# Expert stage of a fused attention and mixture kernel: first-layer sums on three rotating PSUM banks, the second layer's chain a with one alternating bank

## The chip, the cores and the metric

The kernel runs on one core of a Trainium2 chip. The metric is the device time of one execution in microseconds (us). Each time is the median of several executions; one further execution is profiled, and everything that is said of single instructions comes from that one.

## What is computed

Three stages follow one another: an attention in which a query sees only keys of its own cluster, a dense two-layer block with softplus, and a mixture of eight experts whose weights come from a Sinkhorn normalisation. All is float32. The change is in the last stage, cut here to what matters:

```python
def _moe2_ref(x, w_gate, w1, w2):            # x: 1536 x 512, 8 experts, w1[e]: 512 x 1024
    logits = x @ w_gate
    P = np.exp(logits - logits.max())
    for _ in range(8):
        P /= P.sum(1, keepdims=True) + 1e-09
        P /= P.sum(0, keepdims=True) + 1e-09
        P *= N / E
    for e in range(E):
        h = np.maximum(x @ w1[e], 0.0)
        out += P[:, e:e + 1] * (h @ w2[e])
```

## The kernel before

Each float32 operand is split into a high and a low part, and each product is made of three matmuls (high x high, high x low, low x high). On top of that both layers of an expert use a 2 x 2 block scheme with seven products in place of eight (the table `PROD`), so that sums of blocks are formed before and after.

**Stages.** Up to about 600 us the attention and the dense block run, after that the expert stage. In it the 1536 tokens are two halves of 768; the eight experts run over the first half and then over the second, so there are 16 passes, called experts 0 to 15 here (`k` in the code).

**First layer** (`l1_group`). An expert has four quarters `u`, and a quarter has seven groups, i = 0 to 6, in the order of `PROD`. A group is 6 matmuls of 128 x 128 weights with 384 columns. The groups add into two PSUM chains: chain a takes i = 0, 2, 4, 6, chain b takes i = 1, 3, 5, and i = 3 starts chain b afresh. Between the groups the sums are read: ScalarE copies after i = 0, 2, 3 (line 919, the tiles c0 and c2), VectorE adds after i = 1, 4, 5 (line 929), and a ScalarE Relu after i = 6 (line 927). In the profile chain a is called `l0m`, chain b `l1m` while it holds i = 1 and `l3m` from i = 3 on. A group that adds into a chain has to wait until the reader of the group before is done, and a group that starts a chain has to wait until the last reader of its bank is done.

**Second layer** (`l2_piece`). An expert has 14 steps (seven products, each in two halves p), a step has three pieces t = 0, 1, 2 of 128 tokens, a piece has 6 matmuls with 256 columns. The pieces add into chains a and b again (`Ya0m`, `Ya1m`, `Yb0m`, `Yb1m` in the profile; the digit 0 is the bank of t = 0 and 1, the digit 1 that of t = 2, the tail block). After the second half of a product VectorE scales the sums and adds them to the output (lines 961 and 963); for chain a this is after i = 0, 2, 4, 6, for chain b after i = 1, 3, 5.

**Banks.** PSUM has eight banks. `ps_l` holds `la` and `lb`, one for each chain of the first layer; `ps_y` holds `y0` to `y5`. The second layer's chain a uses y0 and y1 in even experts, y2 and y3 in odd ones; chain b uses y4 and y5. In expert 0, whose second layer has not begun, the first layer's odd quarters use y4 and y5. The gate (`gate`, `gate_max`, `sinkhorn`), which runs during expert 0, uses y2 and y3 for its small results.

**Order.** A list `ev2` of steps with due times is sorted and executed in that order when the kernel is built. The second layer of expert k runs beside the first layer of expert k + 1: one and a half pieces follow each group. Between groups i and i + 2 there are three pieces and one group. The framework then lays out each engine's queue from these steps, by priority and by when a step can run in its own reckoning, and sets the semaphores; copies and adds out of PSUM have a raised priority. Each engine works its own queue in order. VectorE has further work there: sums of blocks (`g_sum`, line 72 and 74), low parts of the hidden values (`g_split`, line 889) and of the weights (`w1_split`, line 840). ScalarE casts the high parts (lines 888, 867, 839). POOL forms the low parts of the second layer's weights (`w2_split`, line 868) and issues some DMAs (line 210).

The part that the change touches most, before it:

```python
if i in (0, 1, 3):
    if k == 0 and v:
        LB[bank] = ps_y.tile([P, FH], F32, tag={"a": "y4", "b": "y5"}[bank], name="l" + nm)
    else:
        LB[bank] = ps_l.tile([P, FH], F32, tag="l" + bank, name="l" + nm)
```

Of the kernel before, what the change touches and what calls it, by code (L numbers as in the profile page):

```python
# [7 lines left out]
F32 = mybir.dt.float32  # L8
# [12 lines left out]
def attention_moe_moe2(ctx, tc, v, qt, kt, centroids, w_in, w_out, w_gate, w1, w2, eye, out, dbg=None):  # L21
# [5 lines left out]
    E = w_gate.shape[1]  # L27
    FE = w1.shape[2]
    P = 128
    NT = S // P  # L30
    HT = NT // 2
    CB = HT * P
# [550 lines left out]
    for i in range(NHALF):  # L583
        g = i // 4
        for t in range(HT):
            n = 6 * i + 2 * t - LEAD
# [6 lines left out]
        for s in range(NT):  # L593
            n = 6 * i + s
# [36 lines left out]
    ps_l = ctx.enter_context(tc.tile_pool(name="ps_l", bufs=1, space=PSUM))  # L631
    ps_y = ctx.enter_context(tc.tile_pool(name="ps_y", bufs=1, space=PSUM))
    FH = S // 2
# [39 lines left out]
    Y = {}  # L673
# [39 lines left out]
    def gtile(shape, tag, b, nm):  # L713
        return ps_y.tile(shape, F32, tag=tag, name=nm) if b else ps_l.tile(shape, F32, tag="lb", name=nm)

    def gate(b, hf):
        lg = gtile([E, CB], f"y{2 + hf}", b, f"lg{b}{hf}")
        for c in range(KC):
            nc.tensor.matmul(
                lg, wg[:, c, :], xt[b][:, c, hf * CB : (hf + 1) * CB], start=c == 0, stop=c == KC - 1  # L720
            )
        if b:
            ls = slot_pool["gp"].tile([E, CB], F32, tag="gl", name=f"ls{b}{hf}", bufs=4)
        else:
            ls = slot_pool["fp"].tile([E, CB], F32, tag="u", name=f"ls{b}{hf}", bufs=2)
        nc.scalar.copy(ls, lg)
        tp = gtile([P, HT, E], f"y{2 + hf}", b, f"lgT{b}{hf}")
        for t in range(HT):
            nc.tensor.transpose(tp[:, t, :], ls[:, t * P : (t + 1) * P], idf[:E, :E])
        nc.vector.tensor_copy(lt[:, b * NT + hf * HT : b * NT + (hf + 1) * HT, :], tp)  # L730
# [3 lines left out]
    def gate_max(ph):  # L734
        if ph == 0:
            nc.vector.tensor_reduce(sm[:, 0:1], lt.rearrange("p t e -> p (t e)"), AX.X, ALU.max, negate=True)
            tp = ps_y.tile([1, P], F32, tag="y2", name="gmT")
            nc.tensor.transpose(tp, sm[:, 0:1], idf)
            g1 = mp.tile([1, 1], F32, tag="g1", name="g1", bufs=1)
            nc.vector.tensor_reduce(g1, tp, AX.X, ALU.min)  # L740
            G["g1"] = g1
            return
        bp = ps_y.tile([P, 1], F32, tag="y3", name="gmB")
        nc.tensor.matmul(bp, ones_f[0:1, :], G["g1"], start=True, stop=True)
        nc.vector.tensor_copy(sm[:, 1:2], bp)
        nc.scalar.activation(Pt, lt, AF.Exp, bias=sm[:, 1:2], scale=1.0)

    def sinkhorn(it, ph):
        n = B * NT
        if ph == 0:  # L750
            rs = mp.tile([P, n], F32, tag="rs", name=f"rs{it}", bufs=1)
            nc.vector.tensor_reduce(rs, Pt, AX.X, ALU.add)
            nc.vector.tensor_scalar(rs, rs, 1e-9, None, ALU.add)
            nc.vector.reciprocal(rs, rs)
            nc.vector.tensor_tensor(Pt, Pt, rs.unsqueeze(2).to_broadcast([P, n, E]), ALU.mult)
            cs = G["cs"] = mp.tile([P, E], F32, tag="cs2", name=f"cs{it}", bufs=1)
            nc.vector.tensor_reduce(cs, Pt.rearrange("p t e -> p e t"), AX.X, ALU.add)
            return
        cs = G["cs"]
        cp = ps_y.tile([P, E], F32, tag=f"y{2 + it % 2}", name=f"cp{it}")  # L760
        nc.tensor.matmul(cp, ones_f, cs, start=True, stop=True)
        nc.vector.tensor_scalar(cs, cp, 1e-9, float(E) / N, ALU.add, ALU.mult)
        nc.vector.reciprocal(cs, cs)
        nc.vector.tensor_tensor(Pt, Pt, cs.unsqueeze(1).to_broadcast([P, n, E]), ALU.mult)
        if it == 7:
            nc.vector.tensor_scalar(Nt, Pt, -1.0, None, ALU.mult)
# [34 lines left out]
    W1U, XG, GH, WH, YA = {}, {}, {}, {}, {}  # L801
# [90 lines left out]
    LB = {}  # L892

    def l1_group(k, u, i):
        xn, wn, bank = PROD[i]
        p, v = divmod(u, 2)
        nm = f"{i}m{k}_{u}"
        if i in (0, 1, 3):
            if k == 0 and v:
                LB[bank] = ps_y.tile([P, FH], F32, tag={"a": "y4", "b": "y5"}[bank], name="l" + nm)  # L900
            else:
                LB[bank] = ps_l.tile([P, FH], F32, tag="l" + bank, name="l" + nm)
        ps = LB[bank]
        hi, lo = XC[f"2_{k // E}", xn]
        wh, wl, s_ = W1U[k, u][wn]
        n, nk = 0, KC // 2
# [8 lines left out]
        if i in (0, 2, 3):  # L915
            tag = "c2" if i == 2 else "c0"
# [4 lines left out]
        name = {1: "A11", 4: "A22", 5: "A12", 6: "A21"}[i]  # L921
# [11 lines left out]
    def l2_piece(k, i, p, t):  # L933
        sb, e = divmod(k, E)
        ch = PROD[i][2]
        if p == 0 and t == 0 and i in (0, 1, 3):
            o = 4 if ch == "b" else 2 * (k % 2)
            YA[ch] = [ps_y.tile([P, 512], F32, tag=f"y{o + n}", name=f"Y{ch}{n}m{k}_{i}") for n in range(2)]
        y = YA[ch]
        ps = y[t // 2][:, t % 2 * 256 : t % 2 * 256 + 256]  # L940
        (gh, gl), (wh, wl) = GH[k, i, p], WH[k, i, p]
# [12 lines left out]
        for t_ in ((0, 1) if t == 1 else (2,)):  # L954
            m = r * HT + t_
# [51 lines left out]
    for k in range(NB):  # L1007
# [26 lines left out]
        for i in range(7):  # L1034
            b, i_ = divmod(7 * k + i - 3, 7)
            do(split_at[b][2 * i_ + 1] + 0.15 if b >= 0 else -1, w2_load, k, i)
        for j in range(14):
            i, p = divmod(j, 2)
# [21 lines left out]
    for n, u in enumerate(m1):  # L1060
# [22 lines left out]
        if final:  # L1083
            for hf in range(2):
                gate(0, hf)
# [51 lines left out]
```

## Time and profile before

| | before |
|---|---|
| median of three runs | 1608.32 us (1608.15 to 1611.47) |
| the profiled execution | 1613.91 us |
| its span, first to last instruction | 1612.1 us |
| TensorE matmuls: busy, count | 1518.6 us (94%), 9873 |
| VectorE busy | 1244.7 us (77%) |
| ScalarE busy | 1006.5 us (62%) |
| POOL busy | 725.5 us (45%) |
| mean granted TensorE clock | 0.979 |

How to read it: PE is TensorE's matmuls and PEld its weight loads, DVE is VectorE, ACT is ScalarE. Matmuls are pipelined and their ends are modelled, so the busy time of PE says little; the distance between the starts of two matmuls says when TensorE stood. A wait is given as "engine line waited for: us in total, times, longest". L910 is line 910 of the kernel: the first layer's matmuls; L945 are the second layer's.

### The profile page before, as it was taken

How to read it: one execution, taken by the hardware profiler on the slowest of the kernel's cores; microseconds unless marked ns; L12 is line 12 of the kernel's file. 1: busy time of each engine (PE TensorE's matmuls, PEld its weight loads, DVE VectorE, ACT ScalarE, POOL GpSimd, SP SyncE). 2: the span in 40 equal slices, each digit the busy share in tenths (PEclk: the TensorE clock that was granted, in tenths of full speed). 3: DMA queues.
4: the chain of work that ended last, by engine and by line, in shares of the span. 5: the costliest groups of instructions: out<-in, count | busy, mean ns of one | idle time of the engine just before them, and what ended most of it. 6: DMA issues, size and time to landing. Idle time of an engine off the chain costs nothing. (4 is left out here: it accounts for less than half of the span.)

```text
span 1612.1 us, 26967 instructions
## 1 busy us (share of the span) xinstructions
PE 1518.6 (94%) x9873; PEld 1442.9 (90%) x9873; DVE 1244.7 (77%) x1826; ACT 1006.5 (62%) x1854; POOL 725.5 (45%) x546
## 2 busy tenths in 40 slices
PE   5889999898998999999999999999999999999998
PEld 4778888797988967899999999998999999999998
DVE  4899999865655356977887887898878878878877
ACT  3788888665555535556655665665566666666663
POOL 2322323433323125555665565565445445545544
PEclk7999999899999999999999999999999999999999
DMA  8555520499998406888988887533544443443422
GB/s 220 143 148 140 135 65 6 128 242 248 249 253 227 112 16 173 213 208 223 244 219 218 214 235 209 154 105 112 160 121 123 125 125 118 125 132 110 128 72 79
DMA packets 268532, 253.01 MB, mean 157 GB/s; under 512 B 12272, under 2 KB 235632, under 8 KB 268400
## 3 DMA queue, kind: packets, MB, share of 16 engines
q1 hardware_dynamic: 242656, 217.67, 44.5%
q0 software_dynamic: 25600, 33.56, 12.9%
q8 instruction: 77, 1.26, 0.3%
q14 instruction: 55, 0.45, 0.1%
q10 hardware_dynamic: 144, 0.07, 0.0%
HBM read 194.10 MB, written 36.70 MB: 143 GB/s over the span
## 5 line engine op out<-in xcount | busy, mean ns | idle before, releaser
L868 POOL TENSOR_TENSOR vl<-w2r,vh 128x512 fp32r<-128x512 f32 x224 | 362.3, 1620 | 410.7 <-ACT vh L867 406.3
L889 DVE TENSOR_TENSOR gl<-XA,gh 128x768 fp32r<-128x768 f32 x160 | 175.4, 1096 | 81.9 <-ACT gh L888 81.8
L888 ACT CAST gh<-XA 128x768 fp32r<-128x768 f32 x160 | 134.1, 838 | 108.9 <-PE Ya1m L945 94.5
L945 PE MATMUL Ya0m<-vh,gl 128*128 128x256 f32 x512 | 144.2, 282 | 0.7 <-DVE gl L889 0.7
L867 ACT CAST vh<-w2r 128x512 fp32r<-128x512 f32 x224 | 137.7, 615 | 10.3 <-PE y L688 6.7
L945 PE MATMUL Ya0m<-vh,gh 128*128 128x256 f32 x512 | 144.0, 281 | 0.0
L945 PE MATMUL Ya0m<-vl,gh 128*128 128x256 f32 x512 | 143.9, 281 | 0.0
L210 POOL DMA_DIRECT2D ts<-in_moe_w_dram x48 | 61.9, 1330 | 108.6 <-DMA ts<-in_moe_w_dram 33.9
L945 PE MATMUL Yb0m<-vh,gh 128*128 128x256 f32 x384 | 108.5, 283 | 2.4 <-DVE x L963 2.4
L945 PE MATMUL Yb0m<-vl,gh 128*128 128x256 f32 x384 | 108.6, 283 | 2.0 <-POOL vl L868 2.0
L548 DVE TENSOR_TENSOR el<-t,eh 128x384 fp32r<-128x384 f32 x192 | 102.6, 550 | 10.0 <-ACT eh L544 8.8
L509 DVE TENSOR_REDUCE sc<-s 128x1 f32<-128x768 f32 x96 | 91.2, 951 | 23.4 <-PE s L501 23.2
L945 PE MATMUL Yb0m<-vh,gl 128*128 128x256 f32 x384 | 108.8, 283 | 0.4 <-DVE gl L889 0.4
L931 ACT ACTIVATE XA<-XA 128x768 f32<-128x768 f32 x96 | 81.3, 847 | 38.9 <-DVE XA L929 38.9
L544 ACT CAST eh<-t 128x384 fp32r<-128x384 f32 x192 | 91.6, 481 | 21.4 <-PE t L541 12.3
L541 PE MATMUL t<-idf,E 128*128 128x128 f32 x576 | 97.6, 276 | 4.7 <-ACT OHT L449 2.8
L945 PEld LDWEIGHTS Ya0m<-vh,gl 128*128 128x128 f32 x512 | 97.0, 189 | 1.1 <-DVE gl L889 1.1
L945 PEld LDWEIGHTS Ya0m<-vh,gh 128*128 128x128 f32 x512 | 96.8, 189 | 0.0
L945 PEld LDWEIGHTS Ya0m<-vl,gh 128*128 128x128 f32 x512 | 96.8, 189 | 0.0
L514 ACT ACTIVATE E<-s,sc 128x768 f32<-128x768 f32 x96 | 87.2, 909 | 14.7 <-DVE sc L509 13.6
L72 DVE TENSOR_TENSOR XS<-XA,XA 128x768 f32<-128x768 f32 x32 | 63.9, 1998 | 32.3 <-ACT XA L927 32.3
L541 PEld LDWEIGHTS t<-idf,E 128*128 128x128 f32 x576 | 73.1, 142 | 14.5 <-ACT OHT L449 3.6
(252 smaller groups left out, 5311.8 us busy)
## 6 DMA issues: line engine op xcount, KB each, us to landing
w2r<-td SPq DMA_DIRECT2D x64, 512.0 KB, 4.0
w2r<-in_moe_w_dram SPq DMA_DIRECT2D x56, 512.0 KB, 4.2
ts<-in_moe_w_dram POOLq DMA_DIRECT2D x48, 512.0 KB, 7.7
td<-ts SPq DMA_DIRECT2D x48, 512.0 KB, 5.7
wf<-td SPq DMA_DIRECT2D x64, 256.0 KB, 3.9
w1r<-td SPq DMA_DIRECT2D x64, 256.0 KB, 3.4
AT<-HL SPq DMA_DIRECT2D x64, 192.0 KB, 4.0
ts<-in_moe_w_dram SPq DMA_DIRECT2D x24, 512.0 KB, 6.0
```

The costliest lines, as they stand in the source:

```text
L72: eng.tensor_tensor(out_, a, b, op)
L509: nc.vector.tensor_reduce(SC[i][:, 0, j, t : t + 1], Et[i, t][:, :, 0:CB], AX.XY, ALU.max, negate=True)
L514: nc.scalar.activation(e.rearrange("p (a c) -> p a c", a=2), Et[i, t][:, :, 0:CB], AF.Exp, bias=sc[:, 0, j, t : t + 1], scale=1.0, accum_o ...
L541: nc.tensor.transpose(pt[:, t * P : (t + 1) * P], Et[i, t][:, s * P : (s + 1) * P], idf)
L544: nc.scalar.copy(eh, TT[i, s])
L548: nc.vector.tensor_tensor(el, TT.pop((i, s)), EHL[i, s].bitcast(F32), ALU.subtract)
L867: nc.scalar.copy(h, src)
L868: nc.gpsimd.tensor_tensor(l, src, h.bitcast(F32), ALU.subtract)
L888: nc.scalar.copy(h, src)
L889: nc.vector.tensor_tensor(l, src, h.bitcast(F32), ALU.subtract)
L931: nc.scalar.activation(t, t, AF.Relu, scale=1.0 if name == "A11" else -1.0)
L945: nc.tensor.matmul(ps, g[:, v, ts], w[:, v, :], start=i in (0, 1, 3) and p == 0 and v == 0 and n == 0 and t != 1, stop=p == 1 and v == 1 a ...
```

## The change

Three edits in the expert stage:

- The first layer's sums take one of three banks, `la`, `lb` and `y1`, each time a chain is started. The place is counted on: within a quarter i = 0, 1 and 3 take three banks one after the other, and the next quarter begins one bank further. Expert 0 does the same.
- The second layer's chain a has y0 in even and y2 in odd experts for its first two blocks, and y3 for the tail block in every expert. Chain b stays on y4 and y5.
- The small results of the gate and the normalisation move from y2 and y3 to y4 and y5.

```diff
     def gate(b, hf):
-        lg = gtile([E, CB], f"y{2 + hf}", b, f"lg{b}{hf}")
+        lg = gtile([E, CB], f"y{4 + hf}", b, f"lg{b}{hf}")
...
-        tp = gtile([P, HT, E], f"y{2 + hf}", b, f"lgT{b}{hf}")
+        tp = gtile([P, HT, E], f"y{4 + hf}", b, f"lgT{b}{hf}")
...
-            tp = ps_y.tile([1, P], F32, tag="y2", name="gmT")
+            tp = ps_y.tile([1, P], F32, tag="y4", name="gmT")
...
-        bp = ps_y.tile([P, 1], F32, tag="y3", name="gmB")
+        bp = ps_y.tile([P, 1], F32, tag="y5", name="gmB")
...
-        cp = ps_y.tile([P, E], F32, tag=f"y{2 + it % 2}", name=f"cp{it}")
+        cp = ps_y.tile([P, E], F32, tag=f"y{4 + it % 2}", name=f"cp{it}")
...
         if i in (0, 1, 3):
-            if k == 0 and v:
-                LB[bank] = ps_y.tile([P, FH], F32, tag={"a": "y4", "b": "y5"}[bank], name="l" + nm)
-            else:
-                LB[bank] = ps_l.tile([P, FH], F32, tag="l" + bank, name="l" + nm)
+            tag = ("la", "lb", "y1")[(4 * k + u + (0, 1, 0, 2)[i]) % 3]
+            LB[bank] = (ps_y if tag == "y1" else ps_l).tile([P, FH], F32, tag=tag, name="l" + nm)
...
         if p == 0 and t == 0 and i in (0, 1, 3):
-            o = 4 if ch == "b" else 2 * (k % 2)
-            YA[ch] = [ps_y.tile([P, 512], F32, tag=f"y{o + n}", name=f"Y{ch}{n}m{k}_{i}") for n in range(2)]
+            tags = ("y4", "y5") if ch == "b" else (("y0", "y2")[k % 2], "y3")
+            YA[ch] = [ps_y.tile([P, 512], F32, tag=g, name=f"Y{ch}{n}m{k}_{i}") for n, g in enumerate(tags)]
```

## Rows read from the trace of the kernel before

**Rows 1.** The page: granted TensorE clock in 40 equal slices, tenths of full speed.

```profile
PEclk7999999899999999999999999999999999999999
```

**Rows 2.** Windows, one regular expert; columns: length, busy (x count) per engine, PEclk, DMA.

```profile
1212.73:1272.82 60.09, 60.02 (x421) 59.23 (x420) 48.67 (x64) 38.09 (x66) 30.04 (x21) 1.00 0.41 123
```

**Rows 3.** Waits of TensorE's weight loads, 600 us to the end.

```profile
PEld l3m L910 <- DVE XA L929: 19.4, 32, 3.1
PEld l0m L910 <- ACT XA L927: 7.8, 29, 1.5
```

**Rows 4.** Timeline of TensorE, expert 10, third quarter; columns: start, duration, engine, operation.

```profile
1242.59 0.28 PE L945 MATMUL Yb0m<-vh,gh 128*128 128x256 f32 x1
1242.87 0.45 PE L910 MATMUL l0m<-chA,whAm 128*128 128x384 f32 x1
1243.15 0.34 PE L910 MATMUL l0m<-clA,whAm 128*128 128x384 f32 x1
1243.33 0.34 PE L910 MATMUL l0m<-chA,wlAm 128*128 128x384 f32 x1
...
1248.94 0.28 PE L945 MATMUL Ya0m<-vl,gh 128*128 128x256 f32 x1
1249.06 0.28 PE L945 MATMUL Ya0m<-vh,gl 128*128 128x256 f32 x1
1249.31 0.44 PE L910 MATMUL l3m<-chS,whBm 128*128 128x384 f32 x1
```

**Rows 5.** Windows of 2 us behind the long stall in expert 4.

```profile
874.00:876.00 2.00, 2.00 (x9) 2.00 (x8) 2.00 (x3) 0.52 (x1) 0.00 (x0) 0.50 0.16 42
```

**Rows 6.** Timelines, expert 10: VectorE's add of i=4, TensorE's start of i=6.

```profile
1252.82 1.74 DVE L889 TENSOR_TENSOR gl<-XA,gh 128x768 fp32r<-128x768 f32 x1 [0.23 <-ACT gh L888]
1254.66 0.56 DVE L929 TENSOR_TENSOR XA<-l0m,c03m 128x384 f32<-128x384 f32 x1
1255.38 0.35 PE L910 MATMUL l0m<-chA,whCm 128*128 128x384 f32 x1
...
1224.28 0.54 DVE L929 TENSOR_TENSOR XA<-l0m,c03m 128x384 f32<-128x384 f32 x1
1225.38 0.34 PE L910 MATMUL l0m<-chA,whCm 128*128 128x384 f32 x1
```

**Rows 7.** Timelines of VectorE and TensorE around the stalls in experts 4 and 2.

```profile
864.06 5.13 DVE L72 TENSOR_TENSOR XS<-XA,XA 128x768 f32<-128x768 f32 x1 [2.45 <-ACT XA L927]
873.43 0.69 PE L910 MATMUL l3m<-chS,whBm 128*128 128x384 f32 x1 [2.88 <-DVE XA L929]
878.21 1.42 DVE L889 TENSOR_TENSOR gl<-XA,gh 128x768 fp32r<-128x768 f32 x1 [1.38 <-ACT gh L888]
879.73 0.56 DVE L929 TENSOR_TENSOR XA<-l0m,c03m 128x384 f32<-128x384 f32 x1
880.78 0.34 PE L910 MATMUL l0m<-chA,whCm 128*128 128x384 f32 x1
...
718.75 0.44 PE L910 MATMUL l3m<-chS,whBm 128*128 128x384 f32 x1 [1.90 <-DVE XA L929]
723.46 0.56 DVE L929 TENSOR_TENSOR XA<-l0m,c03m 128x384 f32<-128x384 f32 x1 [0.65 <-PE l0m L910]
```

**Rows 8.** Timelines: eviction of the tail block and next write to one.

```profile
1213.00 0.47 DVE L961 TENSOR_SCALAR x<-Ya1m,Pt 128x256 f32<-128x256 f32 x1
1215.93 0.28 PE L945 MATMUL Ya1m<-vh,gh 128*128 128x256 f32 x1
...
1085.62 0.28 PE L945 MATMUL Ya1m<-vh,gh 128*128 128x256 f32 x1
1086.65 0.47 DVE L963 SCALAR_TENSOR_TENSOR x<-Ya1m,Pt,x 128x256 f32<-128x256 f32 x1
1092.98 0.38 PE L945 MATMUL Yb0m<-vl,gh 128*128 128x256 f32 x1 [2.04 <-POOL vl L868]
```

**Rows 9.** The page's costliest groups: VectorE's sums of blocks.

```profile
L72 DVE TENSOR_TENSOR XS<-XA,XA 128x768 f32<-128x768 f32 x32 | 63.9, 1998 | 32.3 <-ACT XA L927 32.3
```

## Prediction, made before the changed kernel was run

> **What bounds the kernel now.** I read the page first: TensorE's granted clock is full almost everywhere from 600 us on [rows 1]; an engine kept at that clock hardly rests, so I take the time after 602 us (the expert stage, 1010 us of 1612) for TensorE's, and what can be won there for holes in its row. Next the table of windows, cut at the last Relu (L927) of each expert: one expert takes 60.1 us where nothing disturbs it [rows 2]. Next the timeline of TensorE: undisturbed, a 256-column matmul starts 0.12 us after its predecessor (0.118 over many of them) and a 384-column one 0.17 to 0.18 (0.174) [rows 4]. An expert has 42 x 6 = 252 of the first kind and 28 x 6 = 168 of the second: 252 x 0.118 + 168 x 0.174 = 59.0 us. So a regular expert loses 60.1 - 59.0 = 1.1 us; irregular ones lose up to 7. Last the view of waits, for TensorE's weight loads, which see every stall: the largest sum is i=3 waiting for the VectorE add (L929), 19.4 us in 32 places; next i=0 waiting for the ScalarE Relu (L927), 7.8 us in 29 [rows 3]. Both are waits for a bank, not for data: i=3 needs bank b, which the add of i=1 still reads, and i=0 of the next quarter needs bank a, which the Relu of i=6 still reads.
>
> That view gives the idle time; in starts a stall costs a little more, since the matmul behind it is late too. At 1242.87 the first matmul of i=0 comes 0.28 after its predecessor in place of 0.12, and the second 0.28 later in place of 0.17 [rows 4]: 0.16 + 0.11 = 0.27, where the weight load idled 0.21. Adding 0.07 for each of the 61 places: 19.4 + 7.8 + 4.2 = 31.4 us. The two stalls at 719 and 873 us are followed by some 3 us at half clock (0.50 in 874 to 876 us [rows 5]), where 384-column matmuls start 0.32 apart in place of 0.17: 1.6 and 1.3 us more. **All that the change could remove is so about 34 us.** TensorE's other waits (for data, for POOL, for the second layer's evictions) stay.
>
> **The change, part by part.** *First layer over three banks.* No instruction is added or removed, on any engine. The bank of i=0 is now the one that i=1 used a quarter before, free for most of that quarter; that of i=1 is the one of i=3 and i=5, the same distance as now; that of i=3 is the one of i=0 to i=6 of the quarter before, four groups ago. So the waits of i=0 for the Relu and of i=3 for the add go. Inside a quarter i=6 still waits for the add of i=4 (same chain), and i=2, i=4 and i=5 for ScalarE's copies. **What is late next** is VectorE, which works its queue in order: if it is behind, TensorE now runs on through i=3, i=4, i=5 and meets it at i=6. A removed stall counts only as far as i=6 can come earlier: by the distance from the end of i=4's add to the start of i=6, plus the time that VectorE idled before that add for something that TensorE itself sets free.
>
> Regular experts, third quarter: i=3 starts at 1249.31, 0.25 after its predecessor in place of 0.12 [rows 4], and with the matmul behind it loses 0.25; with i=0 that is 0.52. The add of i=4 ends at 1254.66 + 0.56 = 1255.22 and i=6 starts at 1255.38, so 0.16 is free, and VectorE idled 0.23 before, for a ScalarE cast whose buffer second-layer matmuls set free [rows 6]: 0.39 of 0.52 is kept. First quarter: its two stalls are the rest of the 1.1 us, 0.6; the add of i=4 ends at 1224.82, i=6 starts at 1225.38, VectorE is back to back [rows 6]: 0.56 is kept. The other quarters show no stall. The timeline has the first pattern in 10 experts and the second in 11: 10 x 0.56 + 11 x 0.39 = 9.9 us.
>
> Irregular stalls: the rest, 34.3 - (10 x 0.62 + 11 x 0.52) = 22.4 us, in thirteen places. They come where VectorE is late by itself: the subtraction at 864.06 takes 5.13 us, and i=3 then stands 2.88 us, until 873.43. There i=6 could come 880.78 - 880.29 = 0.49 earlier, plus VectorE's idle 1.38 at 878.21 [rows 7]: 1.9 of 4.2 us (with i=0 and the half clock). At 718.75 (1.90 us idle) VectorE afterwards waits for the matmuls of i=4, 0.65 [rows 7], and i=6 has 2.3 us to spare: nearly all, 3.0 us. At 630 and 906 us VectorE runs back to back up to the add of i=4: nothing, and 0.55. The bounds are 0 and 22.4; the same reading at all thirteen gives 13.1, and I take that.
>
> *Second layer's chain a with one alternating bank.* Its tail block (t=2) now sits in one bank for all experts, so its first matmul waits for VectorE's eviction of the expert before. Today that eviction ends at 1213.47 and the next tail matmul starts at 1215.93 [rows 8]: 2.46 us of cover, 2.2 when TensorE no longer stops at i=0. Eleven of the 15 boundaries have 2.4 or more, one 1.7, one 11. Two have none: at 1085.62 the matmul starts 1.5 us before the eviction ends (1086.65 + 0.47), and at the last expert 0.8. Behind the first comes a wait of 2.04 us for POOL at 1092.98 [rows 8], whose end POOL's own queue sets, so that the delay is hidden; without that cover it costs 1.5. Bounds 0 to 2.3; I take 0.8, the second alone. Queued behind that wait on TensorE is its own stream alone.
>
> *Expert 0 and the gate.* Its odd quarters had two banks of their own and now share the three; there the add of i=5 ends 1.0 us or more ahead of the i=1 that will need its bank, so nothing is added. The small tiles of gate and normalisation move to the banks of chain b, which starts after the last of them: 0, and at most one small VectorE step, under 1 us, were it not so.
>
> **Sum.** 9.9 + 13.1 - 0.8 = 22.2 us. The profiled execution took 1613.9 us (span 1612.1, 1.8 around it): 1591.7 for such a one. The median of the runs is 1608.3, 5.6 lower. What can differ between executions are irregular stalls, 38 us of the 56 that all starts after 602 us lose against 0.118 and 0.174; so I scale their term by 33/38 to 11.3: 20.4 us off the median, **1588 us**.
>
> **The rivals.** (B) VectorE takes back all that is irregular: where it is late, it is late until i=6. For it: 630 and 906 us. Against it: VectorE idles before the add of i=4 in most other places. Then 9.9 - 0.8 = 9: 1599 us. (C) All bank waits vanish, since an earlier TensorE also sets VectorE's inputs free earlier: 34 less, 1574 us. (D) The stalls only move to i=6, regular quarters too, or the build holds the banks as long as before: 1607 us. Against it: the free 0.16 to 2.3 us there. (E) The shared tail bank decides. The order of each queue is laid out anew at build time (today four second-layer matmuls stand ahead of i=0 that the program has behind it). If at an expert's end the eviction came behind two of the subtractions that now follow it, 2.0 us each by the page's mean [rows 9], TensorE would stand 4.0 - 2.2 = 1.8 us at 15 boundaries: 27 us against the 21 that the first layer gives, 1615 us. It decides from an eviction 3.6 us later than now. Against it: today's stands right behind its matmuls' other evictions. (F) More switching between banks makes TensorE's clock swing. In the trace TensorE changes banks at each group, and the granted clock is 1.00 through a whole regular expert [rows 2]; it fell behind the stalls of about 2 us or more alone [rows 5]. If each of the 64 quarters had one stretch like that, 1.3 us, it would cost 83: 1671 us. The Trainium skill has such a rule (TensorE: Matmul & The Clock Gate, section "A second HAM failure mode: psum-queue depth-cycling"): a kernel that cycles through PSUM banks each iteration idles briefly between groups of matmuls, often enough that the clock goes back and forth. The trace does not bear that out for the idles of 0.2 us here.
>
> **Chances.** Forecast 0.52, B 0.20, C 0.10, D 0.08, E 0.07, F 0.03. The range runs from C to a little past B, 1574 to 1603, and leaves out D, E and F: 0.18. A measurement of this kernel can tell about 0.2%, 3.2 us, from no change: faster 0.82, same 0.08, slower 0.10.
>
> **What would show it.** In the new profile: i=0 waiting for L927 gone; i=3 waiting for L929 gone or nearly; i=6 waiting for L929 grown by some 8 us; a regular expert of 59.2 us between last Relus; no half clock near 720 and 874 us; the tail matmul waiting for L963 at one or two boundaries, 1.5 us at most. Wrong would be: waits of i=6 as large as what i=0 and i=3 lost, VectorE's adds standing behind more long operations than now, or tail waits at most boundaries.

## The result and the profile after

The changed kernel took 1590.05 us, median of four runs (1587.52 to 1593.84), beside 1609.89 us for the kernel before on the same chip: a ratio of 0.9883, 95% interval 0.9851 to 0.9914. This ratio is the one on record, formed from all runs of both kernels; the quotient of the two medians is 0.9877. The forecast was 1588 us (1574 to 1603), faster by more than 0.2%. A second set of ten runs of the changed kernel, further down, gave 0.9901 (0.9870 to 0.9932).

The profiled execution took 1587.52 us, its span is 1585.7. In the changed kernel's lines the first layer's matmul is L908 (L910 before), its ScalarE copies L917, its Relu L925, VectorE's adds L927, the second layer's matmul L943, its evictions L959 and L961 (L961 and L963 before). Cut at the last Relus of experts 9 and 10, the window view answers to [rows 2] (length, then busy time and count of PE, PEld, DVE, ACT, POOL, then clock, DMA share, GB/s):

```profile
1195.33:1254.50 59.17, 59.17 (x422) 59.05 (x421) 47.73 (x65) 37.92 (x66) 31.99 (x20) 1.00 0.41 125
```

A regular expert went from 60.09 to 59.17 us; 59.2 was forecast. The waits of TensorE's weight loads after 590 us answer to [rows 3]:

```profile
PEld l0m L908 <- DVE XA L927: 16.1, 12, 3.2
PEld cp L761 <- DVE cs L757: 4.3, 3, 1.7
PEld Ya1m L943 <- DVE x L961: 3.1, 2, 2.2
```

In the kernel before the line of i=6 was:

```profile
PEld l0m L910 <- DVE XA L929: 5.6, 6, 3.1
```

Neither i=0 waiting for the Relu (7.8 us before) nor i=3 waiting for the add (19.4) is left. The first line of the changed kernel is i=6 waiting for the add of i=4, in the chain that the change leaves alone: 5.6 us in 6 places before, 16.1 in 12 now. Its third line is the shared tail bank.

**Where the time went.** I cut both profiles at the start of the last Relu of each expert. From the first matmul of expert 0 to the end ("the stage") before took 1009.9 us and after 991.5, 18.4 less. The spans differ by 26.4; the other 8.1 us lie ahead of the stage, where each engine runs the same instructions in the same order. Over the fourteen profiles of this study the stage began between 594.2 and 603.7 us, the kernel before at 602.3 and 598.6, the changed one at 594.2 and 603.7. So that part belongs to no kernel, and I compare stages. The 18.4 us by place, beside the forecast's own terms:

| | before | after | less | forecast |
|---|---|---|---|---|
| regular experts 3, 6, 10 to 15 | 480.2 | 472.8 | 7.4 | 7.6 (8 x 0.95) |
| experts 1, 2, 4, 5, 7, 8, 9 | 447.5 | 440.1 | 7.4 | 15.4 (13.1 and what is left of 9.9) |
| expert 0 | 42.3 | 42.7 | -0.4 | 0 |
| last second layer, after the last Relu | 39.9 | 36.0 | 3.9 | -0.8 |
| sum | | | 18.3 | 22.2 |

The regular term was right, the irregular one twice too large, and a gain that nobody forecast stands at the very end. The irregular row also differs between two profiles of one kernel: it is 445.7 us in e1 (the kernel before again) and 441.0 in e11 (the changed kernel again), so that this pair gives 4.7 in place of 7.4.

### The profile page after: what moved, and what is told of

Read it like the earlier page. It is cut to its first block, busy times and chain, and to the rows that moved or that the text cites. A ratio compares the mean times of both kernels' runs of the same rounds, so it can differ in the third digit from the quotient of the medians.

```text
span 1585.7 us, 26969 instructions
## 1 busy us (share of the span) xinstructions
PE 1501.1 (95%) x9873; PEld 1435.5 (91%) x9873; DVE 1239.9 (78%) x1826; ACT 1004.4 (63%) x1854; POOL 757.1 (48%) x546
## 4 chain that ended last, share of the span: by engine, by line
PE 71%; DVE 14%; DMA 6%; ACT 4%; issue 3%; POOL 1%; SPq 0%; DVEq 0%; ACTq 0%; POOLq 0%
PE l0m L908 15%; PE Ya0m L943 10%; PE Yb0m L943 8%; PE l3m L908 7%; PE Ya1m L943 5%; PE y L688 4%; PE Yb1m L943 4%; PE l1m L908 4%; PE p L654 4%; PE av L556 3%; PE s L501 3%; PE t L541 3%; DMA td<-ts 2%; DMA ts<-in_moe_w_dram 2%; DVE gl L889 2%
## 5 line engine op out<-in xcount | busy, mean ns | idle before, releaser
L868 POOL TENSOR_TENSOR vl<-w2r,vh 128x512 fp32r<-128x512 f32 x224 | 392.5, 1757 | 353.9 <-ACT vh L867 347.6
L889 DVE TENSOR_TENSOR gl<-XA,gh 128x768 fp32r<-128x768 f32 x160 | 166.1, 1038 | 81.5 <-ACT gh L888 80.8
L943 PE MATMUL Ya0m<-vh,gl 128*128 128x256 f32 x512 | 144.6, 282 | 1.8 <-DVE gl L889 1.8
L943 PE MATMUL Ya0m<-vh,gh 128*128 128x256 f32 x512 | 144.3, 282 | 0.0
L943 PE MATMUL Ya0m<-vl,gh 128*128 128x256 f32 x512 | 144.3, 282 | 0.0
L943 PE MATMUL Yb0m<-vh,gl 128*128 128x256 f32 x384 | 108.2, 282 | 0.4 <-DVE gl L889 0.4
L509 DVE TENSOR_REDUCE sc<-s 128x1 f32<-128x768 f32 x96 | 91.0, 949 | 22.4 <-PE s L501 22.2
L943 PE MATMUL Yb0m<-vl,gh 128*128 128x256 f32 x384 | 108.1, 281 | 0.4 <-POOL vl L868 0.4
L943 PE MATMUL Yb0m<-vh,gh 128*128 128x256 f32 x384 | 108.0, 281 | 0.0
L943 PEld LDWEIGHTS Ya0m<-vh,gl 128*128 128x128 f32 x512 | 97.4, 190 | 2.0 <-DVE gl L889 2.0
L943 PEld LDWEIGHTS Ya0m<-vl,gh 128*128 128x128 f32 x512 | 97.0, 190 | 0.0
L943 PEld LDWEIGHTS Ya0m<-vh,gh 128*128 128x128 f32 x512 | 97.0, 190 | 0.0
```

What stands on the lines that cost most here:

```text
L509: nc.vector.tensor_reduce(SC[i][:, 0, j, t : t + 1], Et[i, t][:, :, 0:CB], AX.XY, ALU.max, negate=True)
L868: nc.gpsimd.tensor_tensor(l, src, h.bitcast(F32), ALU.subtract)
L889: nc.vector.tensor_tensor(l, src, h.bitcast(F32), ALU.subtract)
L943: nc.tensor.matmul(ps, g[:, v, ts], w[:, v, :], start=i in (0, 1, 3) and p == 0 and v == 0 and n == 0 and t != 1, stop=p == 1 and v == 1 a ...
```

## The experiments

The stage, the sum of experts 1 to 9 (last Relu to last Relu), a regular expert (11) and the last second layer are read from each profile in the same way; the ratio is the one on record, formed from all runs of both kernels on the same chip, and differs from the quotient of their medians by up to 0.001.

| run | ratio (95%) | stage | experts 1-9 | regular | last layer 2 |
|---|---|---|---|---|---|
| before (profile shown) | | 1009.9 | 567.7 | 60.1 | 39.9 |
| after (profile shown) | 0.9883 (0.9851 to 0.9914) | 991.5 | 558.5 | 59.17 | 36.0 |
| e1_before_again | 1.0007 (0.9982 to 1.0031) | 1008.0 | 565.9 | 60.1 | 39.9 |
| e2_tail_only | 0.9988 (0.9970 to 1.0007) | 1008.5 | 570.3 | 60.1 | 36.0 |
| e3_i0_only | 1.0026 (1.0007 to 1.0046) | 1016.5 | 577.2 | 60.1 | 36.6 |
| e4_i3_only | 0.9922 (0.9896 to 0.9947) | 997.0 | 560.3 | 59.77 | 36.0 |
| e5_before_sp_loads | 0.9925 (0.9905 to 0.9945) | 1004.2 | 560.3 | 60.1 | 39.9 |
| e6_after_sp_loads | 0.9815 (0.9795 to 0.9835) | 982.1 | 548.6 | 59.17 | 36.0 |
| e7_after_tail_free | 0.9906 (0.9882 to 0.9931) | 995.5 | 560.8 | 59.17 | 37.7 |
| e8_after_w1_pool | 1.0136 (1.0116 to 1.0156) | 1036.3 | 582.9 | 62.4 | 36.0 |
| e9_i6_apart | 0.9795 (0.9750 to 0.9841) | 978.5 | 547.6 | 58.99 | 36.0 |
| e10_w1_vector | 0.9830 (0.9787 to 0.9874) | 982.2 | 546.9 | 59.54 | 36.0 |
| e11_after_again | 0.9901 (0.9870 to 0.9932) | 992.5 | 559.5 | 59.17 | 36.0 |
| e12_w1_vector_1to9 | 0.9831 (0.9798 to 0.9865) | 983.0 | 549.9 | 59.17 | 36.0 |

**The parts apart: e1, e2, e3, e4.** e1 is the kernel before, unaltered. e2 has the second layer's tail bank of the change and nothing of the first layer's rotation; e3 and e4 have all of the change but let only i=0, or only i=3, take a bank of its own from expert 1 on.

```diff
+            if k:
+                tag = ("la", "y1")[u % 2] if i == 0 else "lb"      # e3
+                tag = {0: "la", 1: "lb", 3: "y1"}[i]               # e4
```

> The kernel before once more, to see what of the difference between two profiled executions is the execution's and not the change's. In the two profiles at hand the first-layer matmuls begin at 602.3 us before and at 594.2 us after, though the order of each engine's queue is the same up to there. Theory (the 8.1 us are the execution's own, in the attention): this profile begins them anywhere from 594 to 602 us, and from there to the end takes 1010 us within 3. Rival (the change itself makes the stages ahead faster): 602 us again within 1. Ratio to before 1.000 within 0.002.

> Only the second layer's part of the change: the tail block of chain a in one bank for all experts, the first layer on its two banks as before, the gate's small results on y1 and y2. Theory (2.2 to 2.5 us of cover at most boundaries): a regular expert stays at 60.1 us, the tail matmul waits for VectorE's eviction at one or two boundaries only, 1 to 3 us in all, ratio 1.000 to 1.002. Rival (the shared bank costs at each boundary): waits at most of the 15 boundaries, a regular expert above 60.5 us, ratio 1.004 or more.

> The change, but from expert 1 on only i=0 changes banks (la and y1 in turn), while i=1 and i=3 both use lb: the wait of i=0 for the Relu goes, the wait of i=3 for the add of i=1 stays. Theory (a removed stall counts only as far as TensorE does not meet VectorE's queue next): in the third quarter the add of i=1 ends when VectorE's chain from the Relu ends, whatever TensorE does, so i=3 stands 0.5 us there in place of 0.25, and a regular expert is at 60.1 us, 59.9 at the least; i=3 waits for L927 in over 30 places; ratio 0.998 to 1.001. Rival (each bank wait is worth its own length): 2 x 0.27 less, 59.55 us for a regular expert, ratio 0.993 to 0.995.

> The change, but from expert 1 on the three banks are fixed: i=0 in la, i=1 in lb, i=3 in y1. The wait of i=3 for the add of i=1 goes, the wait of i=0 for the Relu (of i=6, in la) stays. Theory (VectorE's queue): i=0 stands 0.27 us in two quarters as before, i=3 nowhere; since i=6 has 0.39 and 0.56 us to spare in the two quarters, all of 0.25 + 0.33 is kept: a regular expert at 59.55 us, and nearly all irregular gain too: ratio 0.990 to 0.993. With the run that changes i=0 alone this tells whether the two parts add up (0.54 + 0.58 = 1.1 of the 0.95 that both gave) or whether the one is worth something only with the other. Rival (each bank wait is worth its own length): the same 59.55 us here, but 59.55 there too.

The tail bank alone is worth nothing that can be measured (0.9988). A bank for i=0 alone, with the tail bank, makes the kernel slower, if by little (1.0026, 1.0007 to 1.0046); a regular expert stays at 60.1 us. The waits of e3's weight loads show the wait for the Relu gone and the wait of i=3 grown from 19.4 to 27.3 us, and its timeline shows why.

```profile
PEld l3m L910 <- DVE XA L929: 27.3, 30, 3.6
PEld l0m L910 <- DVE XA L929: 6.7, 6, 3.1
...
1280.32 0.94 DVE L72 TENSOR_TENSOR XA<-XA,XA 128x768 f32<-128x768 f32 x1
1281.19 0.54 DVE L929 TENSOR_TENSOR XA<-l1m,c00m 128x384 f32<-128x384 f32 x1
1281.79 0.44 PE L910 MATMUL l3m<-chS,whBm 128*128 128x384 f32 x1 [0.34 <-DVE XA L929]
```

i=3 of expert 11 starts 7.08 us after the last Relu of expert 10 here (1281.79 - 1274.71) and 7.07 in the kernel before (1279.41 - 1272.34, not shown): VectorE's add of i=1 sets the time, whether TensorE rested at i=0 or not. With a bank for i=3 alone the stage is 11.5 us shorter than with the tail bank alone (997.0 to 1008.5), but a regular expert gains 0.33 us only, where I had expected 0.55. What is left are the two stalls at i=0 and a new one at i=6 of 0.24 in the third quarter. Waits and timeline of e4:

```profile
PEld l0m L910 <- DVE XA L929: 13.2, 19, 3.3
PEld l0m L910 <- ACT XA L927: 8.6, 30, 1.4
...
1297.72 1.97 DVE L889 TENSOR_TENSOR gl<-XA,gh 128x768 fp32r<-128x768 f32 x1
1299.79 0.56 DVE L929 TENSOR_TENSOR XA<-l0m,c03m 128x384 f32<-128x384 f32 x1
1300.40 0.45 PE L910 MATMUL l0m<-chA,whCm 128*128 128x384 f32 x1
```

The parts don't add: alone they are worth nothing (i=0) and 0.33 us (i=3) of a regular expert, together 0.93.

**What makes VectorE late: e5, e6, e8.** In e5 (on the kernel before) and e6 (on the changed one) POOL issues no adding transfers in the expert stage; the sums of weights that they would form are left out:

```diff
-        if what[0] == "+":
+        if what[0] == "+" and pool == "fp":
             nc.gpsimd.dma_start(t, src, accum_op=ALU.add)
```

> The kernel before, but POOL issues no DMA in the expert stage: the 32 adding DMAs that form sums of expert weights there are plain loads on SP's queue (this leaves the additions out, so the weights of experts 5 to 8 are not the right ones; loads and their sizes stay). Theory (VectorE is late in experts 1 to 7 where its two-input operations meet POOL's DMA issues and POOL's own subtractions): the irregular part of the first layer's bank waits goes, experts 2 to 6 take 300.5 to 303 us together in place of 311.7, and the stage ends 6 to 12 us earlier. Rival (the irregular stalls come from the transfers themselves or from the block sums' place in VectorE's queue): experts 2 to 6 stay above 309 us.

> The same on the changed kernel: POOL issues no DMA in the expert stage, the sums of expert weights are left out there. Theory: experts 2 to 6, which take 303.8 us now, come to 296 to 298 (59.2 each), and of the distance between the two kernels what is left is the regular 0.9 us of each expert, some 15 us from expert 1 to the end with the tail. Rival: above 302 us.

Experts 2 to 6 together: 304.8 us in e5 (311.7 before, 308.8 in e1) and 298.8 in e6 (303.8 after). In both, experts 3 to 6 are regular, 60.1 and 59.2 us each; both sums are 1 to 2 us above the range that I expected, and all of that lies in expert 2 (64.4 and 62.1 us, as with the transfers). Its long operation is another one, a 2.61 us subtraction beside POOL's weight subtraction (L840). So the adding transfers explain experts 4 and 5 and not expert 2. The two runs take away their issue on POOL and the adding itself; that it is the issue is read from the rows. VectorE and POOL in expert 4, in the changed kernel and in e6:

```profile
854.53 1.19 POOL L210 DMA_DIRECT2D ts<-in_moe_w_dram  x1
855.28 1.77 POOL L210 DMA_DIRECT2D w2r<-in_moe_w_dram  x1
856.07 2.85 POOL L840 TENSOR_TENSOR wlCm<-wf,whCm 128x768 fp32r<-128x768 f32 x1
857.89 2.27 POOL L868 TENSOR_TENSOR vl<-w2r,vh 128x512 fp32r<-128x512 f32 x1
855.86 5.12 DVE L72 TENSOR_TENSOR XS<-XA,XA 128x768 f32<-128x768 f32 x1 [2.45 <-ACT XA L925]
```

```profile
855.06 1.85 POOL L840 TENSOR_TENSOR wlCm<-wf,whCm 128x768 fp32r<-128x768 f32 x1 [0.95 <-ACT whCm L839]
856.87 2.01 POOL L868 TENSOR_TENSOR vl<-w2r,vh 128x512 fp32r<-128x512 f32 x1
855.41 2.32 DVE L72 TENSOR_TENSOR XS<-XA,XA 128x768 f32<-128x768 f32 x1 [2.46 <-ACT XA L925]
```

VectorE's sum of two blocks takes 0.95 us where POOL runs nothing beside it. In e6 it ends 0.82 us after POOL's L840. In the changed kernel two DMA issues stand ahead of L840 in POOL's queue, L840 and L868 follow one behind the other, and VectorE's sum ends 0.82 us after the second (857.89 + 2.27 = 860.16; 855.86 + 5.12 = 860.98). It is 5.12 us long and makes VectorE late for the rest of the quarter. The Trainium skill (SBUF — State Buffer, section "Who interferes with whom") has this rule: an instruction of VectorE with two inputs in SBUF contends with one of GpSimd that reads SBUF, the port pair that they share is an exclusive lock, and the order of issue decides who stands. The rows here agree for single meetings; why VectorE did not get its turn between the two subtractions, as it did in e6, no run here shows.

e8 gives POOL VectorE's part of the weights' low parts, so that VectorE has eight operations (8.8 us) less in each expert.

```diff
-            (nc.gpsimd if ch == "C" or k == 0 else nc.vector).tensor_tensor(
+            nc.gpsimd.tensor_tensor(
```

> The changed kernel with the low parts of the first layer's weights (line 840, chunks A and B, 0.7 to 1.3 us each, two in a quarter) formed by POOL in place of VectorE in all experts. Theory (what is left is VectorE's queue up to the add of i=4): two of the operations between the adds of i=1 and i=4 go, the add of i=4 ends some 2 us earlier, the waits of i=6 fall from 16 us to under 6, ratio to before 0.980 to 0.985. Rival (POOL gets longer, and each of its subtractions makes one of VectorE's longer, or the second layer's weights come late): waits for POOL's vl or wl appear, ratio 0.990 or more.

It is 1.4% slower than the kernel before. The window of its expert 10, its waits at i=6, and its line of the costliest groups for VectorE's subtractions:

```profile
1226.83:1289.26 62.43, 59.52 (x422) 59.10 (x421) 47.84 (x57) 38.09 (x65) 43.38 (x28) 1.00 0.39 119
...
PEld l0m L908 <- DVE XA L927: 53.6, 30, 6.7
...
L889 DVE TENSOR_TENSOR gl<-XA,gh 128x768 fp32r<-128x768 f32 x160 | 221.0, 1387 | 99.4 <-ACT gh L888 99.2
```

VectorE has 57 operations in place of 65 and is busy for as long as before (47.84 us, 47.73 in the changed kernel): the same subtractions take 1387 ns on average in place of 1038, because POOL is busy 43.4 us in place of 32.0. So VectorE's lateness here comes from meeting POOL: it has fewer operations and is later.

**The meeting point: e9.** Here i=6 starts a chain of its own in the bank of i=1. The groups i=0, 2 and 4 are so left out of its sum: this is a probe and no version to use.

```diff
-        if i in (0, 1, 3):
-            tag = ("la", "lb", "y1")[(4 * k + u + (0, 1, 0, 2)[i]) % 3]
+        if i in (0, 1, 3, 6):
+            tag = ("la", "lb", "y1")[{0: 0, 1: 1 + u % 2, 3: 2 - u % 2, 6: 1 + u % 2}[i]]
...
-                    start=i in (0, 1, 3) and n == 0,
+                    start=i in (0, 1, 3, 6) and n == 0,
```

> The changed kernel, but group i=6 starts a chain of its own, in the bank that i=1 used (the quarters take turns: the place of i=1 and i=6, and that of i=3 and i=5, change from quarter to quarter). It leaves the sum of i=6 with the groups i=0, 2 and 4 out, so its hidden values differ; the number and size of all instructions stay. In the changed kernel i=6 is where TensorE meets VectorE's add of i=4: 16.1 us in 12 waits, and 0.19 us of each regular expert. Here i=6 needs no reader at all, and the next group that needs the add of i=4 is the i=0 of the next quarter, one group of 1 us and its pieces later (about 2 us). Theory (VectorE's lateness is a matter of a few us and is caught up within a quarter): what was waited for at i=6 goes but for the two or three longest stalls: the stage from the first matmul of expert 0 to the end, 991.5 us in the profile of the changed kernel, becomes 976 to 982; regular experts 59.0. Rival (VectorE is late for good in these places, so the time comes back at the next meeting: at i=0 or i=1, at the low parts gl, or at an eviction): the stage stays within 3 us of 991.5, and the waits carry other names with the same sum.

```profile
PEld cp L761 <- DVE cs L757: 7.3, 4, 2.9
PEld Ya1m L943 <- DVE x L961: 5.9, 2, 5.0
...
PEld l0m L908 <- DVE XA L927: 1.6, 2, 1.3
```

The stage is 978.5 us, 13 less than in the changed kernel, as the theory had it; regular experts are 58.99, about the 58.97 that 252 x 0.118 + 168 x 0.174 gives. Of 16.1 us of waits 1.6 stay, and 5.8 come back elsewhere (3.0 for the normalisation's small sums, 2.8 for the tail bank). So i=6 is where TensorE meets VectorE in the changed kernel, and one group more of slack takes in most of VectorE's lateness.

**The tail bank: e7.** The last expert's tail block gets a bank of its own (`lb`, free by then), so that it need not wait for the eviction of the expert before.

```diff
+            if k == NB - 1 and i == 0:
+                tags = (tags[0], "lb")
```

> The changed kernel, but the last expert's tail block of chain a lies in the bank lb, which nothing needs any more then, so that its first matmul does not wait for the eviction (0.9 us at 1552 us of the changed kernel). From the last Relu to the end the profiles have 39.9 us in both of the kernel before and 36.0 in the three with the shared tail bank and the new tags. Theory (the short wait shifts TensorE and ScalarE against POOL, and VectorE's operations there no longer start just behind POOL's): without the wait the tail takes 39.9 us again, though it waits for less. Rival (the tail is shorter for another reason, the freed bank saves its 0.9 us): 35.1 to 36.0 us.

The wait of 0.7 us at 1552.48 us is gone, and the last second layer is 1.7 us longer (37.7 to 36.0): neither the 39.9 us of the theory nor the rival's 36.0 at most. The timelines of VectorE and POOL just behind that place show it, first the kernel before:

```profile
1576.44 2.08 DVE L74 SCALAR_TENSOR_TENSOR XS<-XS,XA 128x768 f32<-128x768 f32 x1
1580.49 3.64 DVE L889 TENSOR_TENSOR gl<-XS,gh 128x768 fp32r<-128x768 f32 x2
...
1576.40 1.30 POOL L868 TENSOR_TENSOR vl<-w2r,vh 128x512 fp32r<-128x512 f32 x1 [0.70 <-ACT vh L867]
...
1588.98 0.35 PE L945 MATMUL Yb0m<-vh,gh 128*128 128x256 f32 x1 [2.43 <-DVE x L963]
```

The changed kernel:

```profile
1553.91 0.94 DVE L74 SCALAR_TENSOR_TENSOR XS<-XS,XA 128x768 f32<-128x768 f32 x1
1556.82 1.81 DVE L889 TENSOR_TENSOR gl<-XS,gh 128x768 fp32r<-128x768 f32 x2
...
1554.82 10.75 POOL L868 TENSOR_TENSOR vl<-w2r,vh 128x512 fp32r<-128x512 f32 x4 [1.65 <-ACT vh L867]
```

e7:

```profile
1558.82 2.12 POOL L868 TENSOR_TENSOR vl<-w2r,vh 128x512 fp32r<-128x512 f32 x1 [0.73 <-ACT vh L867]
1558.84 0.94 DVE L74 SCALAR_TENSOR_TENSOR XS<-XS,XA 128x768 f32<-128x768 f32 x1
1559.70 2.05 DVE L72 TENSOR_TENSOR XA<-XA,XA 128x768 f32<-128x768 f32 x1
...
1570.63 0.36 PE L948 MATMUL Yb0m<-vh,gh 128*128 128x256 f32 x1 [2.36 <-DVE x L966]
```

In the kernel before POOL starts 0.04 us ahead of VectorE's sum and VectorE stands; its operations are doubled again and again, until chain b waits 2.43 us for an eviction. In the changed kernel POOL's next subtraction, which waits for a cast of ScalarE's, comes 0.9 us later (5.09 us after the last Relu in place of 4.17), VectorE is first, and now POOL stands (four subtractions of 1.3 us take 10.75) while VectorE keeps its pace. In e7 POOL is back at 4.17 us, 0.02 ahead of VectorE's sum, yet here POOL's operation is the one that is stretched (2.12 us) and VectorE's is stretched one operation later; chain b waits 2.36 us. So the small wait is what sets POOL back by 0.9 us, and e2, which has the tail bank alone, has the same 36.0 us. Of the 3.9 us 1.7 are lost again without the wait; the other 2.2 lie between two runs, the kernel before and e7, in which POOL and VectorE start within 0.04 us of each other, and what decides there no run here shows.

**A version that beats both: e10, e12.** e10 goes the other way than e8: POOL's six weight subtractions of an expert go to VectorE from expert 1 on. e12 does so in experts 1 to 9 alone. e11 is the changed kernel again.

```diff
-            (nc.gpsimd if ch == "C" or k == 0 else nc.vector).tensor_tensor(
+            (nc.gpsimd if k == 0 else nc.vector).tensor_tensor(                          # e10
+            (nc.gpsimd if ch == "C" and k > 9 or k == 0 else nc.vector).tensor_tensor(   # e12
```

> The changed kernel, but POOL's part of the weights' low parts (the six subtractions of tile C in an expert, line 840, 7.8 us of POOL's busy time in expert 10 of the changed kernel) goes to VectorE from expert 1 on. Nothing is left out. In the changed kernel VectorE's sums of blocks and low parts take 0.95 us where POOL runs nothing beside them and up to 2.3 us, at POOL's delayed places 5.1, where it does. Theory (what makes VectorE late is meeting POOL, more than its own amount of work): VectorE gets some 4 us of short subtractions an expert but loses the longest meetings (the sum of 2.32 us at each expert's end, the 5.1 us one in expert 4); the regular expert stays at 59.0 to 59.3 and the stage at 991.5 less 2 to 8 us. Rival (VectorE's amount of work decides, 51.4 us of 59.17 already): six more subtractions in its queue make it late at i=6 in every expert: 59.6 us or more a regular expert, the stage 6 us longer or more.

> The changed kernel once more, unaltered, profiled on this chip. Against the question which part of the difference between the profiles of before and after belongs to the change: 18.4 us of it lie behind the first matmul of the expert stage, 8.1 ahead of it, where the queues have the same order. If the 8.1 belong to no change, the start of the expert stage varies from profile to profile (594 to 602 us so far) without regard to the kernel; the regular expert is 59.17 again, the last second layer 36.0, and the stage 991.5 within 4 us, since only the stalls of experts 1 to 8 vary. If they belong to the change, the start is 594 to 595 again and the medians differ by more than the stage does.

> The kernel of the run e10 again, but POOL keeps the subtractions of tile C from expert 10 on (and in expert 0); VectorE has them in experts 1 to 9 alone. Nothing is left out. In e10 the stage took 982.2 us, 9.3 less than in the changed kernel's profile, although each regular expert took 59.53 us in place of 59.17: the gain lay in experts 1, 2, 4 and 7 to 9, where VectorE's longest operation beside POOL was 4.1 us in place of 5.1. Theory (the two effects add: fewer long meetings in the irregular experts, 0.37 us more VectorE work that shows in each regular one): experts 10 to 14 take 59.17 again, experts 1 to 9 stay as in e10 within 3 us in sum, the stage is 982.2 - 6 x 0.37 = 980.0 us, the time 2 us under e10's: 1579 to 1581. Rival (POOL's time in one expert sets how the two meet in the next, so parts of experts can't be taken apart): experts 10 to 15 do not come back to 59.17, or those before 10 change by more than 5 us in sum.

e10 took 1581.72 us (1580.06 to 1583.14) where the changed kernel on the same chip took 1595.34 (1585.94 to 1601.62): every run of e10 is below every run of the other. The stage is 982.2 us, about 10 less. The window of expert 10:

```profile
1185.62:1245.16 59.54, 59.32 (x422) 59.11 (x422) 52.72 (x70) 37.94 (x65) 21.56 (x14) 1.00 0.41 124
```

Both theories had half of it. In the irregular experts fewer meetings win (experts 1 to 9 are 11.6 us shorter than after, and VectorE's longest operation is 4.14 us in place of 5.12), in the regular ones the added work costs 0.37 us each. e12 takes that back, as expected: 59.17 us from expert 10 on, and its experts 1 to 9 are those of e10 but for expert 1 (65.7 to 62.4 us). By that its stage is 983.0 us in place of the 980.0 expected, and its 1583.43 us, just above the 1579 to 1581 expected, can't be told from e10's time. Expert 1 took between 61.4 and 67.8 us over all profiles, 65.7 and 62.4 with the same instructions; what decides there stays open.

## Why the prediction was right, and where it was not

**The regular experts: sum right, shares wrong.** An expert is 0.93 us shorter (60.10 to 59.17), against 0.95 forecast. But the step that gave the third quarter 0.39 and the first 0.56 had it the wrong way round. The timeline of the changed kernel's expert 11:

```profile
1266.52 0.54 DVE L927 TENSOR_TENSOR XA<-l0m,c03m 128x384 f32<-128x384 f32 x1
1267.11 0.44 PE L908 MATMUL l0m<-chA,whCm 128*128 128x384 f32 x1
...
1294.36 0.94 DVE L889 TENSOR_TENSOR gl<-XA,gh 128x768 fp32r<-128x768 f32 x1
1295.41 0.56 DVE L927 TENSOR_TENSOR XA<-l0m,c03m 128x384 f32<-128x384 f32 x1
```

In the first quarter i=6 and the matmul behind it lose 0.19 us. Free between add and i=6 were 0.56 us [rows 6]; the stalls removed ahead of it are 0.61, so i=6 does meet the add, and the matmul behind a late one is 0.11 late as well. The forecast counted the 0.56 and left that last part out. In the third quarter nothing is lost: the subtraction ahead of the add took 1.74 us in [rows 6], beside POOL, and takes 0.94 here. POOL's subtraction runs beside it again, but now it is the one that is stretched (3.00 us from 1293.46). Counted from the last Relu of the expert before, the add comes 1.5 us earlier, 0.8 of it by this; i=6 comes 0.9 earlier. In e4 the same subtraction starts 0.16 us later in the expert (40.02 us after the last Relu of the expert before, in place of 39.86), takes 1.97 us, and i=6 does wait. I had taken VectorE's durations as fixed; they depend on where POOL stands.

**The irregular stalls: mechanism right, the term twice too large.** 15.4 us were forecast for seven experts, 7.4 came (4.7 between e1 and e11). i=6 waits 10.5 us more than before where some 8 were forecast. The failed step is the reading of each stall as it stood, with VectorE's row unmoved. VectorE's row moved, because POOL's did. In expert 2 "nearly all" of 3.0 us was to be kept; POOL's subtraction, which in the kernel before came behind VectorE's sum (0.95 us at 720.08), now starts 0.22 us ahead of that sum, which takes 2.04 us, and i=6 stands 1.64 us. First POOL before, then POOL, VectorE and TensorE of the changed kernel:

```profile
722.69 1.30 POOL L868 TENSOR_TENSOR vl<-w2r,vh 128x512 fp32r<-128x512 f32 x1 [2.82 <-ACT vh L867]
...
713.63 1.45 POOL L868 TENSOR_TENSOR vl<-w2r,vh 128x512 fp32r<-128x512 f32 x1
713.85 2.04 DVE L74 SCALAR_TENSOR_TENSOR XA<-XS,XA 128x768 f32<-128x768 f32 x1
718.20 0.44 PE L908 MATMUL l0m<-chA,whCm 128*128 128x384 f32 x1 [1.64 <-DVE XA L927]
```

In expert 4 the stall that was read behaves as forecast: i=3 no longer stands, and i=6 stands 2.06 us at 870.10. But another stall of i=6 arose ahead of it, at 838.29. There the build has changed POOL's queue: a DMA issue that stood behind one of POOL's subtractions (837.39 before) now stands ahead of it (825.89), and VectorE's two sums behind it take 2.45 and 2.04 us in place of 1.94 and 0.95. In e6, without POOL's issues, expert 4 is regular.

```profile
825.89 1.20 POOL L210 DMA_DIRECT2D ts<-in_moe_w_dram  x1
838.29 0.44 PE L908 MATMUL l0m<-chA,whCm 128*128 128x384 f32 x1 [1.67 <-DVE XA L927]
870.10 0.45 PE L908 MATMUL l0m<-chA,whCm 128*128 128x384 f32 x1 [2.06 <-DVE XA L927]
```

In expert 1 i=6 of the third quarter now stands 3.02 us:

```profile
678.94 2.05 DVE L889 TENSOR_TENSOR gl<-XA,gh 128x768 fp32r<-128x768 f32 x1
...
685.59 0.69 PE L908 MATMUL l0m<-chA,whCm 128*128 128x384 f32 x1 [3.02 <-DVE XA L927]
...
686.00:688.00 2.00, 2.00 (x8) 2.00 (x8) 0.31 (x1) 0.53 (x3) 0.00 (x0) 0.50 0.00 1
```

It starts 48.7 us after the last Relu of expert 0, as it did before (48.8), so that nothing of the stalls removed ahead of it is left; behind it TensorE runs at half clock, and expert 1 takes 65.8 us in place of 64.4 (65.8 in e11, 64.7 in e1). The queues of this expert were laid out in another order by the build, VectorE's too; whether the order or the meeting with POOL makes the stall was not tried. From expert 2 on VectorE's order is the same in both kernels, POOL's too but for the issue named. The errors went both ways: expert 5, where 0.55 us was read off the stall at 906 us, gained 2.7.

**The tail bank.** At two boundaries, as forecast, but 2.02 us and 0.66 in place of 1.5 and 0.8. That the first is hidden behind POOL held in part:

```profile
1071.54 0.38 PE L943 MATMUL Ya1m<-vh,gh 128*128 128x256 f32 x1 [2.02 <-DVE x L961]
...
1077.34 0.39 PE L943 MATMUL Yb0m<-vl,gh 128*128 128x256 f32 x1 [0.39 <-POOL vl L868]
...
1084.40 0.39 PE L943 MATMUL Ya0m<-vh,gl 128*128 128x256 f32 x1 [1.78 <-DVE gl L889]
```

The wait for POOL fell from 2.04 us [rows 8] to 0.39, which is the cover that the forecast named; 7 us later a wait for VectorE of 1.78 us stands that the profile before did not have. e1, the kernel before unaltered, has it too (1.76 us at 1093.81) without any tail wait; there TensorE comes late by a stretch at half clock (0.50 in 1076 to 1082 us), and its wait for POOL is gone. So it may be the price of coming late, whatever the reason; these runs can't tell. Experts 7 and 8 together are shorter all the same (129.0 us to 132.0). The second wait was forecast as a loss of 0.8 and came with a gain of 3.9, of which e7 ties 1.7 to the wait.

**Expert 0, the gate and the clock.** Expert 0 is 0.4 us longer where 0 was forecast. TensorE's waits in the normalisation's small sums grew from 1.5 to 4.3 us; they are waits for VectorE's sums (L757), data and not a bank. Near 720 and 874 us the granted clock now stays at its full level, 2.4 GHz; the half level, 1.2 GHz (0.50 above), appears behind the new 3.02 us stall and behind the wait of 1.78 us at 1084.40. But the forecast's 2.9 us for the half clock were not the kernel's own. In e1 the same stalls of 1.90 and 2.87 us are there, and the clock stays full behind both. Behind the second, in e1 (compare [rows 5]):

```profile
869.00:871.00 2.00, 2.00 (x15) 2.00 (x14) 2.00 (x3) 1.30 (x3) 0.00 (x0) 1.00 0.19 54
```

Experts 2 and 4 take 62.9 and 63.0 us in e1, 64.4 and 64.3 in the profile before. In e11 the half level comes behind the 2.06 us stall of expert 4 (0.50 in 880 to 882 us), and expert 4 takes 64.7 us in place of 63.3. So 1.3 to 1.6 us of an expert's time differ between two profiles of one kernel, with the clock.

**The rivals.** B (nothing of the irregular term is kept) lies nearer than the forecast: of the 13.1 us 5.1 were kept, 2.4 between e1 and e11, when 2.3 us for these experts' other stalls are set aside. C (all waits vanish) is ruled out by the waits at i=6. D (the stalls only move) is what e3 shows for i=0 alone and is wrong for both together. E would need tail waits at most boundaries; there are two. F: the rule of the Trainium skill (TensorE: Matmul & The Clock Gate, section "A second HAM failure mode: psum-queue depth-cycling") that cycling through banks makes TensorE's clock swing is not borne out here, the granted clock is 1.00 through the regular expert. The Trainium skill (Perfetto Trace Analysis, section "Matmuls") also has independent groups rotate through banks, so that one's eviction overlaps the next one's matmuls; the runs agree with the limit that i=0 alone, rotated, was worth nothing (1.0026). That the median came out near the forecast is luck in part: two errors, 8 us too much in the irregular experts and 4.7 too little at the end, had opposite signs. The stage (1009.9 and 1008.0 us to 991.5 and 992.5) is 15.5 to 18.4 us shorter, against 22.2 forecast, and the second set's medians lie 14.3 us apart (1609.67 to 1595.34), against 20.4. The step that took the irregular stalls for all that can differ between executions was wrong as well: the beginning of the stage varies by 9.5 us.

## What to carry over

A wait that is taken away is worth what TensorE can come earlier at its next meeting with the same late engine; free a bank at each meeting, not at one, and look for the last chain that still couples the two (i=6 here, 13 us). Don't treat the durations of VectorE's two-input operations as constants where POOL works beside them: list each one's length against POOL's row, ask where POOL's row goes when TensorE runs earlier, and count a shift of less than a microsecond as able to turn who waits for whom. Compare the order of the queues in both builds, and take two profiles of each kernel before an expert's difference is put down to the change. Moving work from the late engine to its neighbour made it no less busy (e8); moving work the other way was the better kernel (e10).

## What the runs showed of the hardware that I had not expected

VectorE's operations with two inputs from SBUF took at most 0.96 us (128 x 768) with POOL idle and up to 5.1 us beside it. POOL's subtraction of 1.3 us was stretched likewise, four of them to 10.75 us; with POOL 0.9 us later the last second layer was 3.9 us shorter. TensorE's clock fell to 1.2 GHz behind a stall of 2.88 us in one profile of the kernel before and stayed at 2.4 GHz behind the same stall (2.87 us) in another. The beginning of the expert stage varied by 9.5 us between profiles with the same order of all queues ahead of it; what varies there was not tried.
